# Attention scores and values of a pair of heads as unsplit float32 products in the two halves of the array

## The chip, the cores and the metric

The kernel runs on one core of one Trainium2 chip. The metric is the device time of one execution in microseconds; below, "the kernel before" is the kernel without the change. Its time is the median of three runs. Profiles show one execution each. Engines are named as the profile names them: PE is TensorE's matmul, PEld its weight load, DVE is VectorE, ACT ScalarE, POOL GpSimd and SP the engine that issues the DMAs.

## The reference

An attention with a mask by blocks, then two gated layers over all tokens (batch 4, 8 heads, 576 positions, 64 numbers per head; all float32):

```python
scores = scale * np.matmul(q, k.transpose(0, 1, 3, 2))
mask = (pos[:, None] // 64) >= (pos[None, :] // 64)
scores = np.where(mask, scores, -1000000000.0)
attn = softmax(scores)          # with + 1e-09 in the denominator
x = np.matmul(attn, v)          # -> 2304 tokens x 512
g = x @ w_gate                  # 512 x 1536
x = (silu(g) * (x @ w_val)) @ w_out
h = x @ w_in                    # 512 x 2048
out = elu(h) @ w_out2
```

## The kernel before, in words

All dense layers run as three products in the type fp32r: an operand is split into a rounded high part and a remainder (`xh`, `xl`; `wh`, `wl`), and `mm3` issues high by high, remainder by high and high by remainder into one PSUM tile. The 2304 tokens are cut into nine chunks of 256. Chunk 0 holds the first block of every sequence and has an attention of its own (`t0_attn`, untouched but for the names of its PSUM tiles). Chunks 1 to 8 are (batch, half) pairs: half g=0 has 256 queries against 320 keys, half g=1 has 256 queries against 576 keys. Each such chunk has 8 heads, so there are 64 heads, 32 of each half, which stand in 32 pairs.

A head's 256 queries are two tiles of 128: the lower tile (`slo`) sees 192 or 448 keys, the upper one (`shi`) 320 or 576. For each head the kernel computes scores on PE, masks, takes the maximum (DVE), the exponential (ACT), normalises (`norm`, on ACT for the first 48 heads, on DVE for the other 16), transposes the weights on PE in pieces of 128 keys into `tr` (two transposes for a piece, one for the last 64 keys), copies them to SBUF and multiplies by the values into `pv`. The result is split into `xh` and `xl` of its chunk, which the layer `gv` reads.

There are two forms of the two attention products:

- Heads 8 to 63 are split. Queries, keys and values are split by ACT (high part) and POOL (remainder): `ks` holds the high keys in partitions 0 to 63 and the remainder in 64 to 127, `qh` and `ql` likewise hold queries twice, so two fp32r matmuls on the whole 128x128 array give a score tile. The transposed weights are split too (`th` by ACT, `tl` by DVE), and two fp32r matmuls for each piece of keys give the values' product, its two parts in the upper and lower partitions of `pv`, which `xb` and `xf` add.
- Heads 0 to 7 (chunk 1, `NFP = 8`) are whole float32: a score matmul uses 64 rows of the array (the partitions of that head) and all 128 columns; a value matmul uses 128 rows and 64 columns. In the trace each float32 matmul is two records, each with a weight load.

The order on every engine is written out ahead: each step is given to `Plan` with an estimated duration, a due time and the buffers that it reads and writes; `Plan.order` simulates the engines and fixes one order for each. An argument `whole` names PE's mode; the planner charges 100 ns (`SWITCH`) when it changes. `LEAD1`, `LEAD2`, `LEAD` say how much ahead of a chunk's `gv` its attention is due, `CLEAD` and `CSTEP` when the weights are converted (`conv_unit`: DMA, ACT, three steps on DVE, then `wh` on ACT and `wl` on POOL; 24 units for `gv`). `gv` runs chunks 0 and 1 in turns of four of its twelve column blocks, then chunk after chunk; the other layers follow (`y`, then `h` and `o`). `t0_fill` hands PE 62 matmuls on zeros, which stand where the planner finds PE with nothing to do.

Of the kernel before, what the change touches and what calls it, by code (L numbers as in the profile page):

```python
# [22 lines left out]
BLK = 64  # L23
# [105 lines left out]
def attention_moe_moe_kernel(ctx: ExitStack, tc: tile.TileContext,  # L129
                             q0, k0, v0, qf, kf, qt, kt, va, vb, wg, wv, wo, w2i, w2o, out):  # L130
# [82 lines left out]
    def sc_lo():  # L213
        return at_ps.tile([128, 512], F32, tag="slo", name="slo")

    def sc_hi():
        return at_ps.tile([128, 2, 512], F32, tag="shi", name="shi")

    cur = {}

    def tr_t():
        cur["tr"] = at_ps.tile([128, 512], F32, tag="tr", name="tr", bufs=2)
        return cur["tr"]

    def pv_t():
        return at_ps.tile([128, 512], F32, tag="pv", name="pv")


    plan = Plan(dict(raw=3, rawb=2, c=4, rk=2, rq=2, rv=2, ks=3, qh=2, ql=2, vs=3, nm=3, sm=3, pl0=2, pl1=2, ph=2, th=3, tl=3,
                     tt=2, xb=2, xf=2, x=3, slo=1, shi=1, tr=2, pv=1, gv=2, th1=2, s2=2, st=2,  # L230
                     ar=5, ah=3, y=6, ys=4, ws=NW, wm=3, gp=NP, et=2, hc=4))
# [3 lines left out]
    pl_t = {g: [attn.tile([128, e], F32, name=f"pl{g}{i}") for i in range(2)] for g, e in ((0, 256), (1, 512))}  # L235
    ph_t = [attn.tile([128, S], F32, name=f"ph{i}") for i in range(2)]
# [32 lines left out]
    def t0_fill():  # L269
# [7 lines left out]
        for n in range(NFILL):  # L277
            add("PE", 107, lambda n=n: [fill() for _ in range(1 if n else 3)], PFILL, [("wt", 0, 0)])
# [4 lines left out]
    def t0_init():  # L283
# [4 lines left out]
        for i in range(2):  # L288
# [19 lines left out]
    def t0_attn(s, q):  # L308
        tag = ("slo", "pv", "shi", "shi")[2 * s + q]
        sc_k, tr_k, pv_k = (tag, plan.count["shi"] if s and q else nxt(tag), q), ("tr", nxt("tr"), 0), ("gv", nxt("gv"), 0)  # L310
        st, hs, n = {}, range(4 * q, 4 * q + 4), f"0{s}{q}"

        def qk():
            if s == 0:
                t = (sc_lo, pv_t)[q]()
            else:
                if "t" not in t0_sc:
                    t0_sc["t"] = sc_hi()
                t = t0_sc["t"][:, q]
# [78 lines left out]
    NH = B * 2 * H  # L398
    raws, xfs = {}, {}

    def a_pair(n, prio):
        b, g = ORDER[n // H]
        h, i = n % H, n // 2
        ext, nf = (320, 2) if g == 0 else (576, 4)
# [772 lines left out]
```

## Time and profile before

| | us |
|---|---|
| median of 3 runs (range) | 1021.86 (1021.21 to 1023.21) |
| the profiled execution's own time | 1022.86 |
| its span, first to last instruction | 1021.1 |
| PE busy | 1010.5 (99%) |
| PEld busy | 930.3 (91%) |
| DVE busy | 742.6 (73%) |
| ACT busy | 652.6 (64%) |
| POOL busy | 285.2 (28%) |

Attention ends on PE at 448 us and the layer `gv` at 492 us; the layer `y` runs from 461 to 639 us, `h` and `o` from there to the end. A matmul's record is longer than the time for which it keeps the array from the next one, because matmuls are pipelined and their ends are modelled: a 256-column matmul has a record of 0.28 us, but the next one starts 0.12 us after it. So PE's busy share says that it is rarely empty, and the distance from one start to the next says what an instruction costs.

### The profile page before, as it was taken

To read this page: it belongs to the slowest core of one execution; us is meant where nothing else is said; L and a number is where in the kernel's file an instruction comes from. 1 tells how busy PE (TensorE), PEld (TensorE's weight loads), DVE (VectorE), ACT (ScalarE), POOL (GpSimd) and SP (SyncE) were. 2 spreads that over 40 slices of the span, in tenths; PEclk is the share of its full clock that TensorE was granted. 3 is DMA by queue.
4 is the path that set the end of the run, shared out by engine and by line. 5 is a ranking of instruction groups with operands and counts; after the bars stand their busy time and mean duration, and the time that the engine had idled before them with its cause. 6 is when DMAs were issued, how large, how long until landed. Compare 5 with 4: busy or idle time off the path is not lost.

```text
span 1021.1 us, 19137 instructions
## 1 busy us (share of the span) xinstructions
PE 1010.5 (99%) x6542; PEld 930.3 (91%) x6542; DVE 742.6 (73%) x1813; ACT 652.6 (64%) x1645; POOL 285.2 (28%) x291
## 2 busy tenths in 40 slices
PE   9999999999999999999999999999999999999998
PEld 7789999999999999999888889889889989899997
DVE  7899988777777788878766955786986454754554
ACT  6898889888888677653455554655564444654443
POOL 3467535433443344323333322232200000000000
PEclk9999999999999999999999999999999999999999
DMA  6766454323432343015797886887656334353431
GB/s 215 237 209 222 151 180 151 102 84 104 135 115 73 105 125 101 32 64 176 254 340 261 296 323 232 268 264 219 203 155 200 120 114 124 117 176 121 122 105 62
DMA packets 90896, 169.94 MB, mean 166 GB/s; under 512 B 9008, under 2 KB 35120, under 8 KB 90800
## 3 DMA queue, kind: packets, MB, share of 16 engines
q1 hardware_dynamic: 90800, 168.73, 51.5%
q8 instruction: 52, 0.85, 0.4%
q14 instruction: 44, 0.36, 0.1%
HBM read 130.42 MB, written 38.27 MB: 165 GB/s over the span
## 4 chain that ended last, share of the span: by engine, by line
PE 82%; DVE 8%; ACT 4%; DMA 3%; issue 2%; SPq 0%; ACTq 0%; DVEq 0%
PE gv L183 8%; PE gv L184 8%; PE gv L185 7%; PE o L939 6%; PE o L937 6%; PE o L938 6%; PE h L183 5%; PE h L185 5%; PE h L184 5%; PE y L184 5%; PE y L185 5%; PE y L183 5%; PE pv L593 2%; PE pv L592 2%; PE tr L575 2%
## 5 line engine op out<-in xcount | busy, mean ns | idle before, releaser
L183 PE MATMUL gv<-xh,wh 128*128 128x256 f32 x864 | 255.3, 296 | 0.6 <-DVE as L687 0.4
L184 PE MATMUL gv<-xl,wh 128*128 128x256 f32 x864 | 241.3, 279 | 0.0
L185 PE MATMUL gv<-xh,wl 128*128 128x256 f32 x864 | 241.0, 279 | 0.0
L183 PEld LDWEIGHTS gv<-xh,wh 128*128 128x128 f32 x864 | 162.9, 189 | 4.2 <-issue 2.5
L184 PEld LDWEIGHTS gv<-xl,wh 128*128 128x128 f32 x864 | 163.2, 189 | 0.2
L185 PEld LDWEIGHTS gv<-xh,wl 128*128 128x128 f32 x864 | 162.9, 188 | 0.0
L183 PE MATMUL h<-yo,ws 128*128 128x384 f32 x336 | 113.8, 339 | 2.6 <-ACT ys L902 1.2
L185 PE MATMUL h<-yo,ws 128*128 128x384 f32 x336 | 112.8, 336 | 0.0
L184 PE MATMUL h<-yo,ws 128*128 128x384 f32 x336 | 112.7, 335 | 0.0
L898 DVE TENSOR_TENSOR ys<-h,ys 128x384 f32<-128x384 f32 x72 | 40.0, 555 | 68.6 <-ACT ys L902 42.9
L184 PE MATMUL y<-al,woh 128*128 128x512 f32 (+1 forms) x240 | 88.2, 367 | 0.0
L185 PE MATMUL y<-ah,wol 128*128 128x512 f32 (+1 forms) x240 | 88.2, 367 | 0.0
L183 PE MATMUL y<-ah,woh 128*128 128x512 f32 (+1 forms) x240 | 88.2, 367 | 0.0
L848 POOL TENSOR_TENSOR wm<-c,wm 128x256 fp32r<-128x256 f32 x56 | 51.2, 922 | 127.6 <-ACT wm L845 127.5
L891 DVE SCALAR_TENSOR_TENSOR ar<-ar,ar 128x384 f32<-128x384 f32 x96 | 56.5, 589 | 35.3 <-ACT ar L890 34.8
L902 ACT COPY ys<-h 128x384 f32<-128x384 f32 x72 | 34.3, 476 | 74.4 <-PE h L185 73.9
L584 DVE TENSOR_TENSOR tl<-tr,th 128x256 fp32r<-128x256 f32 x176 | 68.9, 415 | 12.0 <-ACT th L580 11.6
L460 POOL TENSOR_TENSOR vs<-rv,vs 128x320 fp32r<-128x320 f32 (+1 forms) x56 | 43.4, 777 | 122.2 <-ACT vs L456 88.6
L889 ACT ACTIVATE ar<-ys 128x384 f32<-128x384 f32 x72 | 37.8, 526 | 59.6 <-DVE ys L898 34.6
L183 PEld LDWEIGHTS h<-yo,ws 128*128 128x128 f32 x336 | 63.1, 188 | 12.1 <-DVE ys L898 3.2
L447 POOL TENSOR_TENSOR ks<-rk,ks 64x576 fp32r<-64x576 f32 (+1 forms) x56 | 68.6, 1226 | 16.4 <-ACT ks L444 7.0
L580 ACT CAST th<-tr 128x256 fp32r<-128x256 f32 x176 | 60.3, 377 | 17.9 <-PE tr L576 16.2
(156 smaller groups left out, 2737.8 us busy)
## 6 DMA issues: line engine op xcount, KB each, us to landing
ws<-w_scr SPq DMA_DIRECT2D x168, 256.0 KB, 2.6
w_scr<-wm SPq DMA_DIRECT2D x56, 256.0 KB, 3.9
a_scr<-as SPq DMA_DIRECT2D x54, 256.0 KB, 2.5
ar<-a_scr SPq DMA_DIRECT2D x48, 256.0 KB, 4.7
rk<-in_kt_dram SPq DMA_DIRECT2D x16, 576.0 KB, 4.1
raw<-in_w2i_dram SPq DMA_DIRECT2D x16, 512.0 KB, 5.3
raw<-in_w2o_dram SPq DMA_DIRECT2D x16, 512.0 KB, 5.1
rq<-in_qt_dram SPq DMA_DIRECT2D x28, 256.0 KB, 3.6
```

What stands on the lines that cost most here:

```text
L183: pe.matmul(dst, wh, xh, start=start, stop=False, skip_group_check=more)
L184: pe.matmul(dst, wh, xl, start=False, stop=False, skip_group_check=more)
L185: pe.matmul(dst, wl, xh, start=False, stop=stop, skip_group_check=more)
L447: pool.tensor_tensor(st["ks"][64:128, 0:ext], raws[i][0][64:128, j, 0:ext], st["ks"][64:128, 0:ext].bitcast(F32), ALU.subtract)
L460: pool.tensor_tensor(v[:, :, 64:128], raws[i][2][:, 0:nf + 1, 64 * j:64 * j + 64], v[:, :, 0:64].bitcast(F32), ALU.subtract)
L580: act.copy(st["th", c], st["tr", c][:, 0:QW])
L584: dve.tensor_tensor(st["tl", c], st["tr", c][:, 0:QW], st["th", c].bitcast(F32), ALU.subtract)
L848: add("POOL", 1000, lambda: pool.tensor_tensor(wm[n][:, 1], part(*x), wm[n][:, 0].bitcast(F32), ALU.subtract), prio, [ck(*x), hk] + whole, ...
L891: add("DVE", 575, lambda: dve.scalar_tensor_tensor(t(), e(), 1.0, t(), ALU.add, ALU.mult), PMP, [tk, ek], [tk])
L937: pe.matmul(d, h, OH[f], start=(p == 0 and u < 2), stop=False)
L938: pe.matmul(d, h, OL[f], start=False, stop=False)
L939: pe.matmul(d, l, OH[f], start=False, stop=(p == HP - 1 and u > 1))
```

## The change

All 64 heads take the float32 form, and the two heads of a pair are computed together. Their queries and keys stand in one tile, head 0 in partitions 0 to 63 and head 1 in 64 to 127. For each piece of keys one score matmul is issued for head 0 in the upper 64 rows of the array and one for head 1 in the lower 64 rows, right behind each other (`a_pair`, `qk`). The value matmuls likewise alternate between the left 64 columns (head 0) and the right 64 columns (head 1) and write the two halves of the partitions of one PSUM tile (`pv`). All splits of queries, keys, values and transposed weights go, and so do `xb` and `xf`. Both score tiles are now of two banks (`sa`, `sb`): a pair with g=0 takes one of them, a pair with g=1 both. Transposes, tails and value products share a tag `tp` of two banks; transposed weights are copied two pieces of keys at a time (512 columns), with eight buffers in place of three. Normalisation is DVE's for all heads (`NACT = 0`). The copies of `k` and `q` in the input hold each head once. The planner's leads and steps have other values. The cores of the diff:

```diff
@@ -32,9 +32,8 @@
 
 PT0, PMP = -1000.0, -500.0
 CV0, CV1, QOUT = PT0 + 1, -20.0, True
-UNIT0, UNIT, LEAD1, LEAD2, LEAD, CLEAD, CSTEP = 3.4, 3.4, 35.0, 10.0, 22.0, 16.0, 1.0
-GF, NACT, NFP, XLP = 4, 48, 8, False
-NPOOL = ()
+UNIT0, UNIT, LEAD1, LEAD2, LEAD, CLEAD, CSTEP = 3.2, 3.4, 25.0, 40.0, 40.0, 20.0, 0.8
+GF, NACT, NTH = 4, 0, 8
 NFILL, PFILL, WARM = 60, 1e9, 3800.0
 EXPS = ((1,1),)
 CLEAD2, CLEAD3 = 8.0, 100.0
...
-    def sc_lo():
-        return at_ps.tile([128, 512], F32, tag="slo", name="slo")
...
-    def sc_hi():
-        return at_ps.tile([128, 2, 512], F32, tag="shi", name="shi")
...
+    def sc_t(tag):
+        return at_ps.tile([128, 1024], F32, tag=tag, name=tag)
+
+    def tp_t():
+        return at_ps.tile([128, 512], F32, tag="tp", name="tp", bufs=2)
...
-    def pv_t():
-        return at_ps.tile([128, 512], F32, tag="pv", name="pv")
...
+    plan = Plan(dict(raw=3, rawb=2, c=4, rk=2, rq=2, rv=3, nm=4, sm=4, pl0=4, pl1=4, ph=4, th=NTH, tt=2, x=3, sa=1, sb=1, tp=2, gv=2,
+                     th1=2, s2=2, st=2, ar=5, ah=3, y=6, ys=4, ws=NW, wm=3, gp=NP, et=2, hc=4))
...
+    pl_t = {g: [attn.tile([128, e], F32, name=f"pl{g}{i}") for i in range(4)] for g, e in ((0, 256), (1, 512))}
+    ph_t = [attn.tile([128, S], F32, name=f"ph{i}") for i in range(4)]
...
+    raws, pair_pv = {}, {}
+
+    def a_pair(i, prio):
+        b, g = ORDER[i // 4]
+        hp = i % 4
...
+        raw = raws[i] = {}
...
+        d0, d1 = prio
+        add("SP", 450, load("rk", [128, S], 2, kt[b, hp, :, 0:ext], lambda t: t[:, 0:ext]), d0, [], [rk], data=1.5 * ext)
+        add("SP", 450, load("rq", [128, QW], 2, qt[g, b, hp], lambda t: t), d0, [], [rq], data=420)
+        add("SP", 450, load("rv", [128, 5, 128], 3, (va, vb)[g][b, hp], lambda t: t[:, 0:nf + 1]), d0, [], [rv], data=200 * (nf + 1))
+
+        sc = {}
+        if g == 0:
+            tag = ("sa", "sb")[i % 2]
+            m = nxt(tag)
+            sks = [(tag, m, 0), (tag, m, 1)]
+        else:
+            sks = [("sa", nxt("sa"), 0), ("sb", nxt("sb"), 0)]
+        pieces = [(0, 1, 0, 320), (320, 0, 0, 192)] if g == 0 else [(0, 1, 0, 512), (512, 1, 512, 64), (576, 0, 0, 448)]
+
+        def qk():
+            if g == 0:
+                t = sc_t(tag)
+                sc.update({j: t[:, 512 * j:512 * j + 512] for j in range(2)})
...
+                sc.update({0: sc_t("sa"), 1: sc_t("sb")})
+            for at, q, o, w in pieces:
+                for j in range(2):
+                    us = slice(64 * j, 64 * j + 64)
+                    pe.matmul(sc[j][:, at:at + w], raw["rq"][us, 128 * q:128 * q + 128], raw["rk"][us, o:o + w], start=True, stop=True)
+
+        add("PE", 1.667 * (e0 + e1) + 45, qk, d0, [rk, rq], sks, whole="q")
+        heads = [a_head(i, j, prio[j], g, sc, sks[j]) for j in range(2)]
...
+        def pv():
+            st["pv"] = tp_t()
+            for c in range(nf + 1):
+                for j, h in enumerate(heads):
+                    x, at, o = (h["th", c // 2], 256 * (c % 2), 0) if c < nf else (st["tt"], 128 * j, 128)
+                    pe.matmul(st["pv"][64 * j:64 * j + 64, o:QW], raw["rv"][:, c, 64 * j:64 * j + 64], x[:, at:at + QW - o], start=c == 0, stop=c == nf)
...
+        add("PE", 225, tr, d1, [h["phk"] for h in heads] + [("id", 0, 0)], [trk], whole=False)
+        add("ACT", 306, cp, d1, [trk], [ttk])
+        add("PE", 427 * nf + 225, pv, d1, [rv, ttk] + [k for h in heads for k in h["thk"]], [pvk], whole="v")
...
+        def xh():
+            x_alloc(ch)
+            act.copy(xh_c[ch][:, hp], st["pv"][:, 0:QW])
+
+        def xl():
+            dve.tensor_tensor(xl_c[ch][:, hp], st["pv"][:, 0:QW], xh_c[ch][:, hp].bitcast(F32), ALU.subtract)
+
+        add("ACT", 307, xh, d1, [pvk], [("x", ch, ("h", hp))])
+        add("DVE", 335, xl, d1, [pvk, ("x", ch, ("h", hp))], [("x", ch, ("l", hp))])
+
+    def a_head(i, j, prio, g, sc, sk):
+        n = 2 * i + j
...
+        nk, sk2 = ("nm", n, 0), ("sm", n, 0)
+        view = lambda u: sc[j][:, 0:e1] if u else sc[j][:, e1:e1 + e0]
+
+        def mask():
+            dve.memset(sc[j][0:64, 128:128 + 2 * e0].rearrange("p (u w) -> p u w", u=2)[:, :, e0 - 64:e0], NEG)
...
+        pl, ph = pl_t[g][nxt(f"pl{g}") % 4], ph_t[nxt("ph") % 4]
+        plk, phk = (f"pl{g}", plan.count[f"pl{g}"], 0), ("ph", plan.count["ph"], 0)
+        Pt, pk = [pl[:, 0:e0], ph[:, 0:e1]], [plk, phk]
...
+        for c in range(0, nf, 2):
+            trk, thk = ("tp", nxt("tp"), 0), ("th", nxt("th"), 0)
+
+            def tr(c=c):
+                t = st["tr", c] = tp_t()
+                for u in range(2):
+                    cs = slice(128 * (c + u), 128 * (c + u) + 128)
+                    pe.transpose(t[:, 256 * u:256 * u + 128], pl[:, cs], ident)
+                    pe.transpose(t[:, 256 * u + 128:256 * u + 256], ph[:, cs], ident)
+
+            def cp(c=c):
+                out["th", c // 2] = attn.tile([128, 512], F32, tag="th", name="th", bufs=NTH)
+                act.copy(out["th", c // 2], st["tr", c])
+
+            add("PE", 450, tr, prio, pk + [("plz", g, 0), ("id", 0, 0), ("fl", 0, 0)], [trk], whole=False)
+            add("ACT", 520, cp, prio, [trk], [thk])
+            out["thk"].append(thk)
+        return out
...
-        for n in range(H * (c - 1), H * c):
-            d = due[c, 0] - (LEAD1 if c == 1 else LEAD2 if c == 2 else LEAD) - (due[c, 0] - due[c - 1, 0]) / H * (H - n % H)
-            if n % 2 == 0:
-                a_pair(n, d)
-            a_head(n, d)
+        lead = LEAD1 if c == 1 else LEAD2 if c == 2 else LEAD
+        for i in range(4 * (c - 1), 4 * c):
+            a_pair(i, [due[c, 0] - lead - (due[c, 0] - due[c - 1, 0]) / H * (H - (2 * i + j) % H) for j in range(2)])
...
+    def pairs(x):
+        return np.ascontiguousarray(x.transpose(0, 1, 3, 2)).reshape(B, 4, 128, x.shape[2])
...
-        "qf": np.ascontiguousarray(q[0, :, BLK:BLK + QW].transpose(0, 2, 1)).reshape(4, 128, QW),
-        "kf": np.ascontiguousarray(k[0, :, :BLK + QW].transpose(0, 2, 1)).reshape(4, 128, BLK + QW),
-        "qt": np.stack([twice(q[:, :, BLK + QW * g:BLK + QW * g + QW]) for g in range(2)]),
-        "kt": twice(k),
+        "qt": np.stack([pairs(q[:, :, BLK + QW * g:BLK + QW * g + QW]) for g in range(2)]),
+        "kt": pairs(k),
```

On PE, in a later chunk, the scores of one split head before, behind matmuls of `gv` and the last value product of its neighbour (`tt` holds the transposed weights of the last 64 keys):

```order
L183 MATMUL gv<-xh,wh_1_1011 128x256
L184 MATMUL gv<-xl,wh_1_1011 128x256
L185 MATMUL gv<-xh,wl_1_1012 128x256
L616 MATMUL pv<-tt,vs 128x128
L478 MATMUL slo<-ks,qh 128x448
L479 MATMUL slo<-ks,ql 128x448
L478 MATMUL shi<-ks,qh 128x288
L479 MATMUL shi<-ks,ql 128x288
L478 MATMUL shi<-ks,qh 128x288
L479 MATMUL shi<-ks,ql 128x288
```

and at such a place of the changed kernel, the values of one pair and the scores of the next (`sa` is head 0's, `sb` head 1's; the values alternate likewise):

```order
L184 MATMUL gv<-xh,wl_1_100 128x256
L452 MATMUL tp<-th,rv 64x256 x8
L452 MATMUL tp<-tt,rv 64x128 x2
L430 MATMUL sa<-rk,rq 128x512
L430 MATMUL sb<-rk,rq 128x512
L430 MATMUL sa<-rk,rq 128x64
L430 MATMUL sb<-rk,rq 128x64
L430 MATMUL sa<-rk,rq 128x448
L430 MATMUL sb<-rk,rq 128x448
L182 MATMUL gv<-xh,wh_1_99 128x256
```

Scores of one head, all on the whole array, have become a block of a pair's values and a block of a pair's scores on half arrays, here one behind the other; over the whole program PE's array changes between its whole form and a half form, or between the two half forms, 45 times before and 100 times now.

On DVE, near the conversion of the eighth unit of `gv`'s weights (the eighth `c` from `raw`, its last step L173 before, L172 now), before:

```order
L173 SCALAR_TENSOR_TENSOR c<-raw_80,c 128x512
L646 TENSOR_TENSOR xl<-pv,xh 64x256
L535 RECIPROCAL sm<-sm 128x2
L512 MEMSET slo 64x64
L171 SCALAR_TENSOR_TENSOR c<-raw_81,c 128x512
L516 TENSOR_REDUCE nm<-slo 128x1
L512 MEMSET shi 64x64
L519 TENSOR_SCALAR nm<-nm 128x1
L516 TENSOR_REDUCE nm<-shi 128x1
L519 TENSOR_SCALAR nm<-nm 128x1
L173 SCALAR_TENSOR_TENSOR c<-raw_81,c 128x512
```

and now, the last twelve instructions up to the same step:

```order
L499 TENSOR_SCALAR sm<-sm 128x2
L464 TENSOR_TENSOR xl<-tp,xh 128x256
L572 TENSOR_TENSOR as<-s_819,gv 128x256
L501 RECIPROCAL sm<-sm 128x2
L478 MEMSET sa 64x2x64
L478 MEMSET sb 64x2x64
L483 TENSOR_REDUCE nm<-sa 128x1
L507 TENSOR_SCALAR pl_128<-pl_128,sm 128x448
L507 TENSOR_SCALAR ph_132<-ph_132,sm 128x576
L170 SCALAR_TENSOR_TENSOR c<-raw_81,c 128x512
L483 TENSOR_REDUCE nm<-sa 128x1
L172 SCALAR_TENSOR_TENSOR c<-raw_81,c 128x512
```

Normalisations and maxima of further heads (here a pair with g=1, `sa` and `sb`) have moved ahead of the conversion: from the start of the program up to that step DVE has 20 normalisations (L507) and 19 maxima (L483) now, against none and 12 before.

## Rows read from the trace of the kernel before

**Rows 1.** The page: the span, and each engine's busy time, share and instructions.

```profile
span 1021.1 us, 19137 instructions
PE 1010.5 (99%) x6542; PEld 930.3 (91%) x6542; DVE 742.6 (73%) x1813; ACT 652.6 (64%) x1645; POOL 285.2 (28%) x291
```

**Rows 2.** Busy time by stretch (instructions), granted clock, DMA share, GB/s.

```profile
0.00:20.00 20.00, 18.00 (x123) 15.96 (x123) 12.89 (x47) 11.79 (x33) 6.45 (x16) 1.00 0.68 235
20.00:40.00 20.00, 20.00 (x120) 14.08 (x119) 18.19 (x57) 17.99 (x54) 7.05 (x6) 1.00 0.56 176
40.00:60.00 20.00, 19.76 (x122) 14.58 (x120) 16.08 (x50) 18.00 (x55) 11.77 (x10) 1.00 0.85 281
60.00:80.00 20.00, 19.40 (x158) 18.47 (x157) 18.93 (x48) 18.95 (x46) 14.02 (x12) 1.00 0.61 206
80.00:100.00 20.00, 20.00 (x165) 19.45 (x165) 18.96 (x51) 17.29 (x45) 15.56 (x13) 1.00 0.60 192
100.00:450.00 350.00, 349.46 (x2924) 345.79 (x2923) 278.66 (x920) 277.09 (x807) 138.38 (x153) 1.00 0.36 112
450.00:500.00 50.00, 49.43 (x389) 47.59 (x389) 40.76 (x70) 22.42 (x47) 18.96 (x14) 1.00 0.49 157
500.00:1021.00 521.00, 514.49 (x2557) 454.35 (x2555) 338.09 (x577) 269.04 (x564) 73.05 (x71) 1.00 0.60 194
```

**Rows 3.** PE's timeline near 49 us, whole float32 heads: start, duration, instruction.

```profile
48.31 0.27 PE L603 MATMUL tr<-ident,ph 128*64 128x128 f32 x1
48.51 1.08 PE L590 MATMUL pv<-th,rv 128*64 128x256 f32 x4
49.52 0.43 PE L614 MATMUL pv<-tt,rv 64*64 64x128 f32 x2
49.88 0.59 PE L476 MATMUL slo<-rk,rq 64*128 64x192 f32 x2
50.30 0.70 PE L476 MATMUL shi<-rk,rq 64*128 64x320 f32 x2
50.93 0.39 PE L183 MATMUL gv<-xh,wh 128*128 128x256 f32 x1
51.16 0.29 PE L184 MATMUL gv<-xl,wh 128*128 128x256 f32 x1
```

**Rows 4.** PE's timeline near 203 us, a split head of g=1.

```profile
202.49 0.37 PE L478 MATMUL slo<-ks,qh 128*128 128x448 f32 x1
202.70 0.36 PE L479 MATMUL slo<-ks,ql 128*128 128x448 f32 x1
202.90 0.28 PE L183 MATMUL gv<-xh,wh 128*128 128x256 f32 x1
...
203.26 0.30 PE L478 MATMUL shi<-ks,qh 128*128 128x288 f32 x1
203.39 0.30 PE L479 MATMUL shi<-ks,ql 128*128 128x288 f32 x1
...
203.79 0.22 PE L616 MATMUL pv<-tt,vs 128*128 128x128 f32 x1
203.85 0.33 PE L183 MATMUL gv<-xh,wh 128*128 128x256 f32 x1
```

**Rows 5.** PE's timeline near 61 us: matmuls on zeros.

```profile
61.28 1.83 PE L274 MATMUL tr<-const-float32-0.0 128*128 128x256 f32 x14
```

**Rows 6.** ACT's timeline (`wh` of the eighth unit); then `gv` alone by stretch, to 48 us.

```profile
42.63 0.63 ACT L176 CAST wh<-c 128x512 fp32r<-128x512 f32 x1
0.00:48.00 48.00, 12.48 (x85) 10.69 (x86) 2.09 (x5) 1.11 (x3) 1.00 0.67 223
```

**Rows 7.** Groups by line and shape: splits that go, a normalisation on DVE.

```profile
L580 ACT CAST th<-tr 128x256 fp32r<-128x256 f32 x176 | 60.3, 377 | 17.9 <-PE tr L576 16.2 <-DVE as L687 0.4
L584 DVE TENSOR_TENSOR tl<-tr,th 128x256 fp32r<-128x256 f32 x176 | 68.9, 415 | 12.0 <-ACT th L580 11.6
L543 DVE TENSOR_SCALAR ph<-ph,sm 128x320 f32<-128x320 f32 x8 | 3.5, 431 | 0.0
```

More of the change, by code (lines that the diff above doesn't have):

```diff
@@ L277, in t0_fill @@
         for n in range(NFILL):
-            add("PE", 107, lambda n=n: [fill() for _ in range(1 if n else 3)], PFILL, [("wt", 0, 0)])
+            add("PE", 107, lambda n=n: [fill() for _ in range(1 if n else 3)], PFILL, [("wt", 0, 0)], [("fl", 0, 0)] if n == NFILL - 1 else [], [("fl", 0, n)])
     def zero(eng, t, a, b):
@@ L287, in t0_init @@
         add("POOL", 900, lambda: make_identity(nc, ident), PT0, writes=[("id", 0, 0)])
-        for i in range(2):
+        for i in range(4):
             add("POOL", 190, lambda i=i: pool.memset(pl_t[0][i][:, 192:256], 0.0), PT0, writes=[("plz", 0, i)])
@@ L531, in rec, with ex @@
+        def ex(u):
+            if "sm" not in st:
+                st["sm"] = attn.tile([128, 2], F32, tag="sm", name="sm", bufs=4)
+            act.activation(Pt[u], view(u), ACTF.Exp, bias=st["nm"][:, u:u + 1], scale=SCALE, accum_out=st["sm"][:, u:u + 1])
         def rec(op):
@@ L543, in norm @@
                 dve.tensor_scalar(Pt[u], Pt[u], st["sm"][:, u:u + 1], None, ALU.mult)
[L545 to L548 removed]
+        add("DVE", 55, mask, prio, [sk], [sk])
+        for u, e in ((1, e1), (0, e0)):
             add("DVE", 1.04 * e + 68, lambda u=u: mx(u), prio, [sk], [nk])
[L550 removed]
+        add("DVE", 69, sc_nm, prio, [nk], [nk])
@@ L551, in a_head @@
+        for u, e in ((1, e1), (0, e0)):
             add("ACT", .833 * e + 240, lambda u=u: ex(u), prio, [sk, nk], [pk[u], sk2])
-        sk2 = [("sm", n, 0), ("sm", n, 1)]
-        add("DVE", 70, lambda: rec(0), prio, sk2, sk2, both=True)
-        add("DVE", 81, lambda: rec(1), prio, sk2, sk2)
+        add("DVE", 70, lambda: rec(0), prio, [sk2], [sk2], both=True)
+        add("DVE", 81, lambda: rec(1), prio, [sk2], [sk2])
         for u, e in ((0, e0), (1, e1)):
-            if n in NPOOL:
-                add("POOL", 1.3 * e + 200, lambda u=u: norm(u), prio, [pk[u]] + sk2, [pk[u]])
-            elif n < NACT:
-                add("ACT", .833 * e + 195, lambda u=u: norm(u), prio, [pk[u]] + sk2, [pk[u]])
-            else:
-                add("DVE", .521 * e + 129, lambda u=u: norm(u), prio, [pk[u]] + sk2, [pk[u]], both=True)
@@ L652, in a_head @@
-        add("DVE", 335, xf, prio, [pvk, K["xb"]], [("xf", i, j)])
-        if j == 1:
-            add("ACT", 307, xh, prio, [("xf", i, 0), ("xf", i, 1)], [("x", ch, ("h", k))])
-            add("POOL" if XLP else "DVE", 790 if XLP else 335, xl, prio, [("xf", i, 0), ("xf", i, 1), ("x", ch, ("h", k))], [("x", ch, ("l", k))], both=True)
+            if n < NACT:
+                add("ACT", .833 * e + 195, lambda u=u: norm(u), prio, [pk[u], sk2], [pk[u]])
+            else:
+                add("DVE", .521 * e + 129, lambda u=u: norm(u), prio, [pk[u], sk2], [pk[u]], both=True)
@@ new lines, in a_head @@
+        out = {"tail": ph[:, e1 - 128:e1], "phk": phk, "thk": []}
+        for c in range(0, nf, 2):
[12 more added lines that the diff above has]
+            out["thk"].append(thk)
```

233 lines of the change are left out of this document (33 added, 200 removed).

## The prediction

> **What bounds the kernel now.** I read the page first: PE is busy for 1010.5 of the span's 1021.1 us, DVE for 742.6, ACT for 652.6 [rows 1]. Busy time of PE says little, since a record outlasts the time for which the array is kept, so I then read PE's timeline for the distance between starts. In an attention stretch a 256-column fp32r matmul keeps PE for 0.12 us, one of 448 columns for 0.205, one of 288 for 0.13, one of 128 for 0.06 [rows 4]. With these, and 0.11 us for a transpose (0.06 for that of a head's last 64 keys), the 2924 matmuls of 100 to 450 us need 342.4 of the 350 us [rows 2], an estimate: 7.6 us are lost to waits in all that stretch. The clock granted is 1.00 in every stretch [rows 2], the upper level of 2.4 GHz. Two places lose more. In the first 20 us PE waits for first loads and fills with zeros; the change leaves that alone. From 60 to 80 us there are 158 matmuls, 14 of them on zeros [rows 2, 5], so 144 real ones against 165 in the next 20 us: about 2.5 us. DVE and ACT are nearly full just there (18.9 of 20 us each) and have room later (279 and 277 of 350) [rows 2]. So PE's own work sets the time; a change that relieves ACT, DVE and POOL is worth its effect on PE's sequence and at most 10 us of waits.
>
> **What a whole float32 product costs on a half array.** Rows 3 hold one head's values and another's scores without a break. In us: four records of 256 columns take 1.01, two of 128 take 0.36, two of 192 take 0.42, two of 320 take 0.63 [rows 3]. From 192 to 320 columns the pair of records grows by 0.21 for 128 columns, 1.64 ns a column, which is four cycles at 2.4 GHz (1.667 ns). Streaming is then 0.853 + 0.213 + 0.32 + 0.533 = 1.92 us. From the transpose ahead (its 0.11 after 48.31) to the end of the extra time of the first `gv` matmul behind (0.23 in place of 0.12) it is 51.04 - 48.42 = 2.62 us. The 0.70 us that are not streaming belong to four changes of the array's form (whole to columns, the tail's 64x64, rows, whole): 0.175 us each.
>
> A rule of the Trainium skill (TensorE: Matmul & The Clock Gate, Part 3, what overlaps and what doesn't) says that a weight load overlaps running matmuls only where the row group differs. The four records of one half in 1.01 us [rows 3] leave 0.157 us beside streaming, form change included, so their loads lie beside matmuls of the same half. By the rule, at an estimate of 0.107 and 0.053 us for a load of 128 and 64 columns (same page, LDWEIGHTS), some 25 us of loads would stand bare; I go by the row.
>
> **The sum, removed.** Heads 0 to 7: streaming 8 x 1.92 = 15.4 us. Split heads with g=1: scores 2 x 0.205 + 4 x 0.133, values 8 x 0.117 + 0.06, together 1.94; 32 of them, 62.0 [rows 4]. Split heads with g=0: scores 2 x 0.09 + 2 x 0.145 (scaled from [rows 4]), values 4 x 0.117 + 0.06, together 1.00; 24 of them, 24.0. Form changes: 45 x 0.175 = 7.9. In all 109.3 us.
>
> **Added.** A pair's score columns are 512 (g=0) or 1024 (g=1) for each head, its value columns 640 or 1152. If the two halves run beside each other, a pair streams for one head's columns: 16 x 1152 x 1.667 ns = 30.7 and 16 x 2176 x 1.667 ns = 58.0, together 88.8 us. Form changes: 100 x 0.175 = 17.5. In all 106.3, so PE's work shrinks by 3.0 us. Per pair: the first four gain about 3.3 us each, having run one half at a time and changed form 11 times; the 28 others lose 0.3 to 0.5 each, because two fp32r passes already cost what two overlapped float32 halves cost, and each block changes the form twice. Whether the halves overlap is shown by no row: before, neighbouring half matmuls are always in the same half. The bounds are 88.8 us and twice that; I take the lower one, as weight loads are already seen to run beside matmuls and the halves share neither rows nor partitions of PSUM, or not the same columns.
>
> The transposes stay as many. Their copies, 192 of 256 columns (0.38 us on ACT [rows 7]), become 96 of twice the width; 176 remainders on DVE (68.9 us [rows 7]) go, and all the splits of keys, queries and values. That is off PE's path and counts only through waits, as do the smaller loads: q and k come once, not twice, in a stretch where DMA is 0.36 busy [rows 2].
>
> **Waits.** Later, 2.5 + 7.6 us can come back; I take 6 of them (0 to 10). Early, the order has a price. Heads 0 to 15 are now normalised by DVE, and 20 normalisations and 7 more maxima stand ahead of the eighth weight unit's last DVE step. At 0.43 us each [rows 7] that is 11.6 us; DVE was idle for 5.7 of 20 to 60 us [rows 2], so the unit comes 6 to 12 us later. Before, its `wh` was done at 43.3 and its first matmul ran at 48 (the 85th of `gv`) [rows 6]: under 5 us to spare. Behind that matmul, on PE, all else is queued. PE reaches it after about the same work as before. I take 4 us (0 to 10).
>
> Sum: -3 + 4 - 6 = -5 us: 1022.86 to 1017.9 by the profiled execution (span 1016). The median is 1.0 under that execution: **1017**.
>
> **Rivals.** (1) Starts in order. The two records of a float32 matmul stand behind each other in one half; if PE starts matmuls strictly in order, head 0's second record, waiting for its half, holds up head 1's first. Then only second and next first record overlap. For g=0 scores this gives 267 + 267 + 267 + 160 + 160 = 1.12 us in place of 0.853; for g=1, with its 64-column piece between, 2.51 in place of 1.71; values take 0.213 more. That is 16 x (0.267 + 0.80) + 32 x 0.213 = 23.9 us, less 3 us of early wait that longer blocks cover: **1038**. It decides the sign alone. For it speaks that all starts of the timeline are in order; against it nothing, since no two halves were in use. The same page of the Trainium skill says that matmuls start and end in program order, which is this case; it also reports 3.07 times for four row tiles and 2.38 for three column tiles, one matmul in each, which no run here shows and which either case would allow.
>
> (2) It doesn't do what it says: the halves run one after the other. Then 88.8 us more streaming, and no early wait: **1102**. The planner would have charged half of what PE takes, and nothing hides it on a full PE. Against it: see above.
>
> (3) Halves overlap, but waits eat it: the early wait is 10 us in place of 4, and nothing comes back later, since one score tile for each head (`sa`, `sb`) makes the next pair's scores wait for both heads' exponentials: **1029**. For it: DVE at 18.9 of 20 us from 60 to 100 us [rows 2]. Against it: a pair with g=1 has about 13 us of PE's time (350 us for 27 or so pairs [rows 2]) and needs its score tiles for some 8 us, an estimate from two scores' maxima and exponentials.
>
> **Chances.** A measurement here tells a difference of 0.2% (2 us) from none. Overlap with these waits 0.58, own range 1009 to 1025 (form changes 0.1 to 0.2 us each, waits at their bounds): faster 0.40, same 0.10, slower 0.08. In order 0.23, one after the other 0.07, waits 0.12: slower but for 0.02 each of faster and same. Together faster 0.42, same 0.12, slower 0.46. The likeliest case is 1017; the range 1008 to 1042 takes in the in-order case and leaves out the serial one.
>
> **What would show it.** In the profile after: a block of scores with g=1 lasting about 1.7 us, and head 1's first record starting before head 0's second (overlap); 2.5 us with head 1 a record late (in order); 3.4 us (serial). A block of values with g=1 at 1.9, 2.1 or 3.8. PE idle or on zeros between 35 and 55 us, behind `wh` of the eighth unit at 48 us or later, shows the early wait; more matmuls than 2924 from 100 to 450 us, less the missing splits, would show waits given back. `y` starting before 461 us, and the distance from there to the end unchanged, would show that the gain is attention's. The prediction is wrong if a form change costs more when both halves were in use, or if DVE's early load stays on PE's path to 120 us.

## The result, and the profile after

The changed kernel takes 1012.2 us (median of four runs, 1011.3 to 1013.3) against 1022.5 for the kernel before beside it (four runs, 1021.2 to 1030.3): a ratio of 0.988, interval [0.984, 0.992]. Forecast were 1017, a range of 1008 to 1042 and a gain of 5 us; the gain is 10.3 by the medians, 11.5 by the profiled executions (1022.86 and 1011.31). The page after, as in [rows 1]:

```profile
span 1009.5 us, 18001 instructions
PE 999.9 (99%) x6598; PEld 888.9 (88%) x6598; DVE 659.1 (65%) x1489; ACT 510.1 (51%) x1193; POOL 129.6 (13%) x127
```

By stretch, with the columns of [rows 2]:

```profile
0.00:20.00 20.00, 19.23 (x140) 18.22 (x141) 14.60 (x50) 11.85 (x34) 6.80 (x20) 1.00 0.79 271
20.00:40.00 20.00, 18.00 (x135) 13.95 (x135) 19.67 (x67) 15.39 (x45) 5.09 (x4) 1.00 0.49 164
40.00:60.00 20.00, 19.65 (x149) 15.83 (x148) 19.34 (x54) 15.79 (x38) 5.23 (x4) 1.00 0.65 203
60.00:80.00 20.00, 19.66 (x175) 17.86 (x173) 18.58 (x35) 12.45 (x27) 9.55 (x8) 1.00 0.78 227
...
100.00:450.00 350.00, 349.71 (x2974) 312.41 (x2973) 194.49 (x607) 153.57 (x424) 8.54 (x8) 1.00 0.27 85
450.00:500.00 50.00, 48.82 (x351) 44.93 (x350) 41.95 (x72) 21.34 (x43) 16.01 (x13) 1.00 0.63 203
```

DVE has become the fullest engine beside PE from 20 to 60 us (39.0 of 40, before 34.3), and from 100 to 450 it has shed 84 us, ACT 124 and POOL 130. The clock is granted at 1.00 throughout, as before.

**The halves overlap.** PE's timeline of one value block with g=1 (a row joins neighbouring records), and of one score block with g=1, record by record (start, duration, instruction):

```profile
183.48 1.95 PE L452 MATMUL tp<-th,rv 128*64 128x256 f32 x16
185.26 0.39 PE L452 MATMUL tp<-tt,rv 128*64 128x128 f32 x4
185.58 0.69 PE L430 MATMUL sa<-rk,rq 64*128 64x512 f32 x1
...
201.86 0.69 PE L430 MATMUL sa<-rk,rq 64*128 64x512 f32 x1
201.87 0.69 PE L430 MATMUL sb<-rk,rq 64*128 64x512 f32 x1
202.40 0.59 PE L430 MATMUL sa<-rk,rq 64*128 64x512 f32 x1
202.40 0.59 PE L430 MATMUL sb<-rk,rq 64*128 64x512 f32 x1
...
203.43 0.54 PE L430 MATMUL sa<-rk,rq 64*128 64x448 f32 x1
203.43 0.54 PE L430 MATMUL sb<-rk,rq 64*128 64x448 f32 x1
203.90 0.39 PE L182 MATMUL gv<-xh,wh 128*128 128x256 f32 x1
```

Head 1's first record starts 0.007 us behind head 0's first (0.01 in the rounded rows), not behind its second. The score block lasts 2.03 us to the first `gv` matmul (1.71 of streaming foretold, and two changes of form), the value block 2.10 (1.92 foretold, and two). All 32 value blocks, and all but two of the score blocks, last what their shape lasts here.

**Where PE's time went.** I gave each distance between two starts on PE to the earlier matmul. A matmul's distance beyond 0.24 us over the usual one of its shape counts as a wait, and so do 1.9 us by which two early score blocks are longer than the others. At the passage from a transpose to an fp32r matmul, which starts 0.08 us early and lasts 0.08 us longer, I moved that 0.08 back. Worked out so, the span closes for both kernels (us, each number rounded by itself):

| PE | before | after | difference |
|---|---|---|---|
| scores, values, transposes | 170.7 | 161.3 | -9.4 |
| `gv` (2592 matmuls) | 306.2 | 304.2 | -2.0 |
| `y`, `h`, `o` | 521.6 | 521.0 | -0.7 |
| matmuls on zeros | 11.0 | 9.7 | -1.3 |
| waits | 6.3 | 8.2 | +1.9 |
| ahead of the first, behind the last start | 5.2 | 5.2 | 0 |
| span | 1021.1 | 1009.5 | -11.6 |

By stretch the waits were 0.3 us from 20 to 60, 2.7 from 60 to 500, 3.3 after 600; after the change 4.8, 2.6 and 0.8. So no waits came back in the attention stretch: there were hardly any to come back. The gain is PE's own work.

A part of it was in no term of the forecast. In a run of `gv` matmuls without a break the distance is 113 ns or 118, and it mostly stays what it is within a run. First and last of 20 starts in such a run of the kernel before, then of the kernel after:

```profile
231.91 0.28 PE L184 MATMUL gv<-xl,wh 128*128 128x256 f32 x1
...
234.15 0.28 PE L185 MATMUL gv<-xh,wl 128*128 128x256 f32 x1
```

```profile
253.80 0.28 PE L183 MATMUL gv<-xl,wh 128*128 128x256 f32 x1
...
255.95 0.28 PE L184 MATMUL gv<-xh,wl 128*128 128x256 f32 x1
```

That is 2.24 us for 19 distances, 118 ns each, and 2.15, 113 each. Before, 250 runs of `gv` held 2084 inner distances, 116.0 ns in the mean, 42% of them at 114 or less; after, attention stands in larger blocks, there are 107 runs, the mean is 114.3 and 78% are at 114 or less. Summed over 113.3 ns each the excess fell from 5.6 to 2.5 us. (More entries from half matmuls give 1.1 of that back, which leaves the 2.0 of the table.) What puts a run in one pace or the other no run here shows.

### The profile page after: what moved, and what is told of

It reads as the page before. It is cut to its first block, busy times and chain, and to the rows that moved or that the text cites. A ratio compares the mean times of both kernels' runs of the same rounds, so it can differ in the third digit from the quotient of the medians.

```text
span 1009.5 us, 18001 instructions
## 1 busy us (share of the span) xinstructions
PE 999.9 (99%) x6598; PEld 888.9 (88%) x6598; DVE 659.1 (65%) x1489; ACT 510.1 (51%) x1193; POOL 129.6 (13%) x127
## 4 chain that ended last, share of the span: by engine, by line
PE 92%; DVE 5%; DMA 1%; ACT 1%; issue 1%; SPq 0%; ACTq 0%; DVEq 0%
PE gv L182 9%; PE gv L183 8%; PE gv L184 8%; PE o L824 6%; PE o L822 6%; PE o L823 6%; PE h L182 6%; PE h L184 6%; PE h L183 6%; PE y L183 5%; PE y L182 5%; PE y L184 5%; PE tp L452 5%; PE sa L430 4%; PE tp L530 2%; PE tp L531 2%
## 5 line engine op out<-in xcount | busy, mean ns | idle before, releaser
L182 PE MATMUL gv<-xh,wh 128*128 128x256 f32 x864 | 249.4, 289 | 0.3 <-DVE as L572 0.3
L567 DVE SCALAR_TENSOR_TENSOR s<-th,gv 128x256 f32<-128x256 f32 x108 | 45.0, 417 | 103.2 <-ACT th L563 102.7
L563 ACT ACTIVATE th<-gv 128x256 f32<-128x256 f32 x108 | 41.8, 387 | 97.9 <-PE gv L184 96.7
L824 PE MATMUL o<-oh,gl 128*128 128x512 f32 x180 | 70.6, 392 | 0.0
L822 PE MATMUL o<-oh,gh 128*128 128x512 f32 x180 | 70.5, 392 | 0.0
L823 PE MATMUL o<-ol,gh 128*128 128x512 f32 x180 | 70.2, 390 | 0.0
L535 ACT COPY th<-tp 128x512 f32<-128x512 f32 x96 | 53.4, 591 | 31.9 <-PE tp L531 31.8
```

The costliest lines, as they stand in the source:

```text
L182: pe.matmul(dst, wh, xh, start=start, stop=False, skip_group_check=more)
L535: act.copy(out["th", c // 2], st["tr", c])
L563: act.activation(st["th"], st["t"][:, 0], ACTF.Tanh, scale=0.5)
L567: dve.scalar_tensor_tensor(st["s2"], st["th"], 1.0, st["t"][:, 0], ALU.add, ALU.mult)
L822: pe.matmul(d, h, OH[f], start=(p == 0 and u < 2), stop=False)
L823: pe.matmul(d, h, OL[f], start=False, stop=False)
```

## The experiments

The expectations were written with the prediction's fixed distances, by which 11 us of waits had come back between 60 and 500 us and PE lost 6.3 us more than before from 20 to 60; the table above was made after them. "367.5 us from the first `h`" in them is a slip: it is the time from the first to the last `h` start of the kernel before. From the first `h` start to the end it is 381.8 us before and 378.2 after.

**All of head 0, then all of head 1.**

```
-            for at, q, o, w in pieces:
-                for j in range(2):
+            for j in range(2):
+                for at, q, o, w in pieces:
...
-            for c in range(nf + 1):
-                for j, h in enumerate(heads):
+            for j, h in enumerate(heads):
+                for c in range(nf + 1):
```

> The changed kernel with one thing different: in each block of scores and of values all matmuls of head 0 are issued first, then all of head 1, where the change has them in turn, head by head. Work, bytes and number of form changes are the same. Theory A (the two halves run beside each other only where their matmuls are neighbours in PE's order, since a matmul that waits for its half holds up all behind it): only the last record of head 0 lies beside the first of head 1, 0.37 us of a block of scores with g=1, 0.16 with g=0, 0.11 of a block of values. Of the 88.8 us of streaming that the overlap saves, 16 x 0.37 + 16 x 0.16 + 32 x 0.11 = 12 us stay and 77 are lost: 1012 + 77 = about 1089, less some us of the early wait that longer blocks cover, so 1083 to 1090; a block of scores with g=1 lasts some 3.1 us in place of 1.7. Theory B (each half has a queue of its own and looks past matmuls of the other half): nothing changes, 1010 to 1014. In between, if a few matmuls can be passed: 1030 to 1070.

Measured: 1054.5 us (one run), 42 more, between the two theories. PE's timeline of a score block with g=1 (a row joins neighbouring records of one tile):

```profile
197.51 1.18 PE L430 MATMUL sa<-rk,rq 64*128 64x512 f32 x3
198.48 0.69 PE L430 MATMUL sb<-rk,rq 64*128 64x512 f32 x1
198.53 0.70 PE L430 MATMUL sa<-rk,rq 64*128 64x64 f32 x2
199.01 0.59 PE L430 MATMUL sb<-rk,rq 64*128 64x512 f32 x1
199.07 0.54 PE L430 MATMUL sa<-rk,rq 64*128 64x448 f32 x1
199.44 1.14 PE L430 MATMUL sb<-rk,rq 64*128 64x64 f32 x4
200.51 0.39 PE L182 MATMUL gv<-xh,wh 128*128 128x256 f32 x1
```

All six records of `sa` stand ahead of `sb` in the program, yet `sb` starts with the third of them: when four of `sa`, the starting one among them, are left. In a value block with g=1 (ten records of a head) it starts with the seventh, again four from the end. So PE goes past up to three records that wait behind the one that has started in their half; a fourth holds up all behind it. Blocks of values with g=1 last 3.44 us in place of 2.10 (head 1 starts six records of 0.216 us later, 1.30), those of scores with g=1 3.00 in place of 2.03, and scores with g=0, four records for each head, stay at 1.07. Together the blocks last 43 us longer, which is all of the difference. Rival 1 of the prediction, strict order, falls for good: there the next half could not start before the last of these records.

The Trainium skill (TensorE: Matmul & The Clock Gate, Part 3, what overlaps and what doesn't) says that matmuls start and end strictly in program order. The rows differ: `sb`'s first matmul starts at 198.48, and `sa`'s third matmul, which stands ahead of it, at 198.64 (the second of the two records that the row from 198.53 joins). Between halves the order holds only to within the few records named above.

**Two of head 0, two of head 1, and so on.**

```
-            for at, q, o, w in pieces:
-                for j in range(2):
+            for p0 in range(0, len(pieces), 2):
+                for j, (at, q, o, w) in [(j, p) for j in range(2) for p in pieces[p0:p0 + 2]]:
```

(and values likewise, by two chunks)

> The changed kernel with matmuls issued two of head 0, then two of head 1, and so on, in place of one and one; work the same. With all of head 0 first, head 1's first record started when head 0 had four records left, the starting one among them: a block of values with g=1 lasted 3.44 us in place of 2.10, six records of 0.216 longer. Theory A (each half has its own queue, four records deep): head 1's first record starts beside head 0's first, blocks last as after the change (2.10, 2.03), time 1010 to 1014. Rival B (four records in all, whichever half they are for): head 1 starts a record late and stays so, blocks of values are 0.2 longer, of scores 0.2 to 0.4, time 1020 to 1026. Rival C (the look-ahead is one of matmuls, not records, or depends on loads of weights): more than 1030.

Measured: 1014.5 us (one run). Blocks of values with g=1 last 2.15 us, of scores 2.04, within 0.05 of the change's; two score blocks with g=0 in a row last 2.03 in place of 1.93. That is what theory A expected; rival B, as it was put (a record late throughout, values 0.2 longer), and rival C are out. It doesn't show that each half has four places of its own: four waiting records in all, head 1's first among them, give the same start in this run (three of head 0 wait, and head 1's) and in the one before (at the third record of six, at the seventh of ten). No run here tells the two apart.

**The plan: the changed kernel with the old numbers, and the old kernel with the new.**

```
-UNIT0, UNIT, LEAD1, LEAD2, LEAD, CLEAD, CSTEP = 3.2, 3.4, 25.0, 40.0, 40.0, 20.0, 0.8
+UNIT0, UNIT, LEAD1, LEAD2, LEAD, CLEAD, CSTEP = 3.4, 3.4, 35.0, 10.0, 22.0, 16.0, 1.0
```

> The changed kernel with the planner's seven numbers of before (UNIT0, UNIT, LEAD1, LEAD2, LEAD, CLEAD, CSTEP = 3.4, 3.4, 35, 10, 22, 16, 1.0); code and matmuls the same, only the order differs (102 changes of the array's form in place of 100). Theory A (what was won comes from the pairs: the work taken from ACT, DVE and POOL removes the waits): at most 3 us above or below 1012, so 1009 to 1015. Rival B (the new plan gives the waits back, by issuing attention earlier than it is needed): the 11 us of waits between 60 and 500 us come back in part or whole, 1017 to 1024. For the stretch from the first h matmul to the end (367.5 us after the change, 3.6 us less than before it, where neither kernel has attention work): if it is the placing of the weights' conversions on DVE and POOL, it moves by some us with the plan alone; if it is the lighter engines, it stays at 367 to 368.

> The kernel before with only the planner's seven numbers of the change (UNIT0, UNIT, LEAD1, LEAD2, LEAD, CLEAD, CSTEP = 3.2, 3.4, 25, 40, 40, 20, 0.8); no pairs, no relief, old buffers. It is the other half of the run of the changed kernel with the old numbers, which took 1033.0 us: 20.8 us more than with the new ones, 6.8 of it between 450 and 500 us, where the weights' conversions for y came late. Theory A (the new numbers alone give the waits back, whatever the kernel): the old kernel gains most of the 11.8 us that it lost between 60 and 500 us, 1009 to 1014. Theory B (the numbers only suit the pairs: without the relief of DVE, ACT and POOL attention can't be run ahead): 1018 to 1026, and it may get longer, as attention issued earlier stands before the conversions on DVE and ACT.

Measured: 1033.0 us for the changed kernel with the old numbers (ratio to before 1.009 [1.008, 1.011]) and 1035.8 for the old kernel with the new ones (1.012 [1.008, 1.016]). Both theories on the first expected less than what came; of the second, B is right in sign and too small. Waits are some 25 and 17 us in these two (with the early score blocks of the first; 8.2 and 6.3 with the plan that fits). By stretch, the changed kernel with the old numbers, then the old kernel with the new:

```profile
100.00:450.00 350.00, 343.04 (x2896) 305.08 (x2895) 190.66 (x597) 147.38 (x411) 2.57 (x2) 1.00 0.27 81
450.00:500.00 50.00, 44.73 (x360) 39.30 (x360) 33.51 (x66) 21.88 (x48) 14.60 (x10) 1.00 0.35 111
```

```profile
60.00:80.00 20.00, 17.08 (x113) 14.79 (x113) 15.99 (x45) 18.60 (x48) 12.05 (x11) 0.91 0.45 151
...
100.00:450.00 350.00, 343.79 (x2832) 335.92 (x2831) 285.23 (x905) 275.71 (x795) 142.82 (x154) 1.00 0.38 114
```

In the first PE waits with DVE at 191 of 350 us, so not for want of an engine's time. That attention comes late and piles up is the likely reason: its last matmul starts at 465.7 us, against 444.3 in the change. The waits name the links, from 100 to 500 us (total us, times, longest):

```profile
PE gv L182 <- DVE as L572: 6.9, 7, 1.4
PE tp L441 <- ACT th L535: 2.5, 3, 1.1
```

In the second, attention run ahead meets an ACT that is busy for 18.6 to 19.4 of every 20 us from 20 to 100 us, and DVE for 16.0 to 19.2; but only 4.4 of its waits lie between 60 and 100 us and 9.2 between 100 and 450, so that this is their cause is argued, not shown. Code and plan can't be told apart by adding: with the old numbers the new code costs 10.5 us more than the old, with the new it takes 23.6 less.

**Which of the numbers.**

```
-UNIT0, UNIT, LEAD1, LEAD2, LEAD, CLEAD, CSTEP = 3.2, 3.4, 25.0, 40.0, 40.0, 20.0, 0.8
+UNIT0, UNIT, LEAD1, LEAD2, LEAD, CLEAD, CSTEP = 3.4, 3.4, 25.0, 40.0, 40.0, 16.0, 1.0
```

> The changed kernel with only those of the planner's numbers set back to before that place the weights' conversions and the units (UNIT0, CLEAD, CSTEP = 3.4, 16, 1.0); the leads of attention stay new (25, 40, 40). With all seven old it took 20.8 us more, which by the starts on PE lie 1.9 between 20 and 60 us, 8.1 between 60 and 450, 6.1 between 450 and 500 and 2.4 after 600. Theory A (attention's leads make the 8.1, the conversions the 6.1 and what is early): 1018 to 1022. Rival B (all of it comes from the leads, as attention that comes late piles up before y): 1011 to 1015. Rival C (all from the conversions): 1030 to 1035.

Measured: 1014.4 us (0.992 [0.990, 0.994]): rival B. With the new leads the old placing of the conversions costs 2 us, so the 20.8 us need the old leads of attention, those of the conversions' stretch too. The old leads with the new placing were not run, and code and plan above did not add, so how much the leads cost alone stays open.

**The relief: the splits' work put back as idle work.** For each head from the ninth on, at its due time:

```
+        for j in range(2) if i >= 4 else ():
+            p, z = prio[j], slice(64 * j, 64 * j + 64)
+            add("ACT", .833 * ext + 93, lambda: act.copy(dA[:, 0:ext], raw["rk"][:, 0:ext]), p, [rk])
+            add("POOL", 2.1 * ext + 250, lambda: pool.tensor_tensor(dP[64:128, 0:ext], raw["rk"][64:128, 0:ext], raw["rk"][64:128, 0:ext], ALU.subtract), p, [rk])
...
+            for u in range(2) if i >= 4 else ():
+                add("DVE", 335, lambda c=c, u=u: dve.tensor_tensor(dD, out["th", c // 2][:, 256 * u:256 * u + 256], out["th", c // 2][:, 256 * u:256 * u + 256], ALU.subtract), prio, [thk])
```

> The changed kernel with the work that the change took from the split heads put back as work whose results nobody reads: for each head from the ninth on, the copies of keys, queries and values on ACT and the subtractions on POOL, and two subtractions of 256 columns on DVE for each copied pair of transposes, all at the due times of their heads. PE's work is the same as after the change. Theory A (waits were given back because ACT, DVE and POOL were relieved): most of the 11.3 us between 60 and 500 us is lost again, 1018 to 1024 us. Rival B (they were given back because a pair of heads is one longer block with four buffers behind it, and the plan issues it early): 1011 to 1015. From the first h matmul to the end 367.5 us by both, as nothing is added there, unless the order of the weights' conversions moves.

Measured: 1061.5 us (1.036 [1.034, 1.039]). Theory A in sign, and more than four times its size: waits are some 42 us (here and below without what single score and value blocks lose).

With ACT normalising 48 heads again as well:

```
-GF, NACT, NTH = 4, 0, 8
+GF, NACT, NTH = 4, 48, 8
```

> The changed kernel with the idle work of the splits on ACT, POOL and DVE, as in the run that took 1061.5 us, and with the normalisations of the first 48 heads on ACT instead of DVE, as they stood before the change: the three engines then carry about what they carried before (DVE some 700 us, ACT some 620, POOL 261), and PE what it carries after. Theory A (the waits were given back by the relief; the 49 us of the run before this came from DVE, which got the idle work and the normalisations): without relief the pairs lose what they gained, 1020 to 1030. Rival B (pairs need engines that answer faster than heads one by one did, since two score tiles free up late): still far above before, 1040 to 1060. Rival C (only DVE counted, the rest of the relief is worth nothing): 1012 to 1016.

Measured: 1048.8 us (1.024 [1.019, 1.029]), in rival B's range: at about the engine loads of the kernel before, PE waits for some 33 us where that kernel waited for 6. Rival B's reason, score tiles that free up late, is not what the waits show; the longest from 20 to 1000 us is for the results of `gv`, and few are for `sa`:

```profile
PE gv L182 <- DVE as L585: 12.5, 6, 3.6
PE tp L541 <- DVE xl L475: 4.0, 4, 2.1
...
PE sa L431 <- ACT pl L506: 1.2, 1, 1.2
```

With the idle work on ACT and POOL alone (NACT = 0; the last two lines of the long diff above left out):

> The changed kernel with the idle copies on ACT and the idle subtractions on POOL for heads from the ninth on, and nothing idle on DVE; normalisations on DVE as in the change. Theory A (it is DVE's relief, 176 remainders, that counts; ACT and POOL had room): 1012 to 1018. Rival B (POOL's work slows DVE's own beside it: in the run with all idle work DVE's normalisations took 0.51 to 0.52 us in place of 0.41 to 0.45, and its 128x2 scaling 0.287 in place of 0.188): a good part of the 49 us is there without any idle work on DVE, 1025 to 1045.

Measured: 1034.4 us (1.010 [1.006, 1.013]), rival B. The groups of DVE's scaling of the maxima and of a normalisation, from 0 to 500 us, in the changed kernel and in this one (its lines stand 11 lower):

```profile
L486 DVE TENSOR_SCALAR nm<-nm 128x2 f32<-128x2 f32 x64 | 11.1, 188 | 0.1
L507 DVE TENSOR_SCALAR pl<-pl,sm 128x192 f32<-128x192 f32 x32 | 10.1, 315 | 0.8
```

```profile
L497 DVE TENSOR_SCALAR nm<-nm 128x2 f32<-128x2 f32 x64 | 20.1, 327 | 0.2
L518 DVE TENSOR_SCALAR pl<-pl,sm 128x192 f32<-128x192 f32 x32 | 15.8, 494 | 0.4
```

That it is POOL can be read instruction by instruction. Of the 64 scalings of this kernel, the 34 that have a POOL instruction beside them for some of their time take 475 ns in the mean, the other 30 take 159, like the 57 that stand alone in the changed kernel; of the normalisations shown, 16 take 672 ns beside POOL and 16 take 316 without. Not all of DVE's work is touched: the maxima over 576 columns of `sb` take 746 ns in both kernels. How much of the 22 us is this and how much the copies on ACT no run separates. And the wait comes early, at a price of its own; this kernel by stretch:

```profile
20.00:40.00 20.00, 15.66 (x106) 11.38 (x106) 16.75 (x50) 15.12 (x45) 9.84 (x10) 0.83 0.40 124
40.00:60.00 20.00, 16.52 (x87) 10.97 (x83) 18.95 (x44) 15.64 (x35) 11.06 (x12) 0.83 0.49 151
```

PE is idle for 7.8 of these 40 us, and the granted clock is 0.83 in the mean of each stretch, part of the time at the lower of its two levels (1.2 GHz), so what PE does there takes longer too: 193 matmuls in place of 284. By the trace the clock first falls at 31.9 us, in a wait of PE from 29.0 to 33.2. The two runs before this one lose by the clock as well (0.97 and 0.99 in the mean from 100 to 450 us): their `gv` matmuls that start at the lower level take 7.0 and 4.6 us more than at 118 ns each.

**Fewer buffers.** Two in place of four for `pl` and `ph`, and:

```
-GF, NACT, NTH = 4, 0, 8
+GF, NACT, NTH = 4, 0, 4
```

> The changed kernel with fewer buffers: two in place of four for the exponentials of each shape (pl, ph) and four in place of eight for the copied transposes (th), as few as a pair can live with; the planner knows of it and orders anew. Theory A (deep buffers let attention run ahead, and that is part of why waits were given back): 1018 to 1030, with PE waiting for th or for exponentials between 100 and 450 us. Rival B (the two score tiles sa and sb and the two transposed tiles in PSUM limit how far it runs ahead anyway): 1011 to 1015.

Measured: 1017.4 us (0.994 [0.992, 0.996]), at the edge of theory A's range, but not in its place: from 100 to 450 us waits are 0.5 us as with deep buffers, from 20 to 100 they are 6.6 in place of 3.3 (without the two early score blocks), and the granted clock is 0.91 from 20 to 40 and from 40 to 60 us (`gv` matmuls at the lower level take 2.4 us more). So buffers count where the first pairs are brought up, not for running ahead.

**The early wait.** Normalisations of the first 16 heads on ACT:

```
-GF, NACT, NTH = 4, 0, 8
+GF, NACT, NTH = 4, 16, 8
```

> The changed kernel with NACT = 16 in place of 0: the normalisations of heads 0 to 15 (32 of them, 0.25 to 0.43 us each) go from DVE to ACT, as they stood before the change; the rest is the same. Theory A (the 6.3 us that PE lost between 20 and 60 us more than before the change come from DVE's early load, through the eighth weight unit): DVE gets about 11 us less to do before 100 us and the loss falls by 3 to 6 us, to 1006 to 1009 us. Rival B (the loss comes from waits for ACT and POOL too, wl at 29.7 and the x parts at 31.4 us, and ACT is itself full there): ACT is 3 to 4 us per 20 us fuller, what DVE gives back ACT takes, and the time stays within 1.5 us of 1012 or gets longer by up to 4.

Measured: 1015.9 us (0.992 [0.991, 0.994]), rival B. Waits from 20 to 60 us rise to 6.7 us (2.8 in the change, counted alike, without its two score blocks), as POOL's `wl` (behind ACT's `wh`) comes late:

```profile
PE gv L184 <- POOL wl L179: 3.5, 4, 1.4
```

Without EPS on the sums of a head:

```
-        add("DVE", 70, lambda: rec(0), prio, [sk2], [sk2], both=True)
```

> The changed kernel without the addition of EPS to the sums of a head (one 128x2 operation on DVE for each of the 64 heads, mean 0.19 us; EPS is 1e-9 and a sum at least 1, so float32 gives the same sum). DVE gets 12 us less, 3 of them for the first 16 heads, while DVE is busy for 39.0 of 40 us from 20 to 60 us. Theory A (the 6.8 us that PE loses there are DVE's load): 2 to 3 us back, 1009 to 1010.5. Rival B (they are the order of the units, POOL's wl and ACT's wh as much as DVE): within 1.5 us of 1012. A new order of the plan may move either by 2.

Measured: 1019.9 us (0.998 [0.996, 0.999]), 7.7 more with less to do, outside both. Waits from 20 to 60 us are 3.1 (2.8 in the change, counted alike), so 3 us less of DVE's work did not shorten them; but the planner, with 64 short steps less, orders all anew, and 3.0 us of waits arise between 100 and 450 us and 2.5 after 600.

The same, and:

```
-GF, NACT, NTH = 4, 0, 8
+GF, NACT, NTH = 4, 4, 8
```

> As the kernel without EPS, and the normalisations of the first four heads go to ACT (NACT = 4; with 16 it took 3.6 us more than with none, ACT being busy for 37.2 of 40 us). Theory A (early work is best shared: DVE 39.0 and ACT 31.2 of 40 us after the change, some 3.5 us moved leaves both near 34 to 36): another 1 to 3 us, 1006 to 1009. Rival B (what ACT has to do before wh counts the same as what DVE has to): 1010 to 1014.

Measured: 1016.7 us (0.994 [0.992, 0.996]), neither. Its waits after 600 us are 4.4 us, although neither of these two edits touches anything there. From the first `h` start to the end the kernels with the change's code take 378.2 (the change, and fewer buffers) to 382.0 us (this one), 380.7 with the old numbers. None of the variants beats the change.

## Why the prediction came out as it did

**Overlap: right.** The lower bound of 88.8 us of streaming was the one to take; the records start side by side, and the serial and the in-order rivals are ruled out by the timeline and by the order of issue. What decided it was not shown by any row before: a record that waits for its half lets those of the other half go ahead, past three of them at the most. Issued head by head, the same matmuls would have made the kernel slower than before, by 32 us.

**PE's work: right in sign, mis-sized.** Forecast -3.0. By the table it is -9.4 for scores, values and transposes, and -2.0 for `gv`. The step that failed is the one on removed work: I priced the split heads by the shortest distances of [rows 4], 86 us. The trace of before has 92 us for those 696 matmuls, 0.7 of it waits (one of 256 columns takes 127 ns in the mean, not 117, as breaks and the slower pace count). And 143 runs of `gv` less, at some 20 ns for where each begins and ends, are another 3. On the added side the changes of form cost about 0.20 us each, not 0.175: 109 in place of 106.3. And `gv`'s pace inside its runs, 3.1 us, had no term at all. With the forecast's -3.0 these make some -12 us, where the two rows have -11.4; a run of `gv` begins and ends in both rows, so the terms don't divide as the rows do.

**Early wait: right in size.** Forecast +4; waits from 20 to 60 us went from 0.3 to 4.8. But only 0.5 of them stands where I put it, so the size agrees by luck. The eighth unit's `wh` was done 9.7 us later, as worked out (6 to 12), and PE, having been given other work, waited 0.5 us for its `wl`. ACT's row, and PE's three longest:

```profile
52.31 0.62 ACT L175 CAST wh<-c 128x512 fp32r<-128x512 f32 x1 [1.26 <-DVE c L172]
```

```profile
30.80 0.39 PE L184 MATMUL gv<-xh,wl 128*128 128x256 f32 x1 [0.85 <-DVE sm L499]
...
32.78 0.33 PE L441 MATMUL tp<-ident,ph 128*128 128x128 f32 x1 [1.15 <-DVE xl L464]
...
54.54 0.39 PE L184 MATMUL gv<-xh,wl 128*128 128x256 f32 x1 [0.35 <-POOL wl L179]
```

The rest are two score blocks (37.4 and 45.9 us) in which `sb` waits for the exponentials of the pair before and holds up `sa` behind it, 1.9 us: rival 3's mechanism, at its place only at the start.

**Later waits given back: the wrong step.** I read 7.6 us of waits between 100 and 450 us out of [rows 2] and [rows 4], and took 6 as coming back. That number was what fixed distances failed to explain; real waits in that stretch were 1.0 us. What came back instead is the longer distances of the two items above, which the change removes because attention stands in fewer and larger blocks. From 60 to 500 us waits went from 2.7 to 2.6, and the 14 zeros of [rows 5] went, against 1.3 us of zeros now from 20 to 25 us.

**Not forecast:** 2.5 us less waiting after 600 us, where the change does nothing. Kernels with one and the same code there differ by up to 3.8 us, so this is the order that the planner happens to give; it is argued from these kernels, not tested by itself.

So the forecast of 1017 stood on one right cause, one right size for another reason, and a term of -6 that was really PE's work mis-priced. That it fell only 5 us short is luck in part: the step that failed, waits taken from what a model left over, happened to have the sign of the work that was priced too low. That relief and plan don't give waits back doesn't make them idle: with either left out, PE of the changed kernel waits for some 23 to 42 us.

## What to carry to other kernels

Two float32 matmuls on different halves of the array run side by side if they are issued in turn, here at most two matmuls (four records) of one half ahead of the other; all of one half first cost 42 us. On a full PE, price removed work by the mean distance that its group really takes, not by its shortest, and count as waits only distances that a row shows as waits; the remainder of a model is not idle time. A change of code and the plan that orders it are to be tried in all four combinations before either is credited.

## What was not expected of the hardware

- A half's records that wait, up to three behind the one that has started, let the other half's first one start ahead of them (197.51 to 198.48 us above).
- A `gv` matmul of 256 columns is 113 or 118 ns from the next, and keeps that pace for long stretches of a run.
- A transpose ahead of an fp32r matmul is followed after 28 ns in place of 109, and the fp32r matmul then takes 201 in place of 118: the passage costs 2 to 3 ns in all.
- With POOL busy for 121 of 350 us in place of 9, DVE's 128x2 scaling takes 327 ns in place of 188, and all of the difference lies on those that POOL's instructions overlap (475 ns against 159).
